# Reversing GpSimd's additions of weight chunks, and placing the last chunks of slots eight and nine anew

## The chip, the core and the metric

The kernel runs on one core of a Trainium2 chip. The metric is the device time of one execution in microseconds (us); the time before is the median of three runs. A core has five engines with a queue each: TensorE (PE in the profile), VectorE (DVE), ScalarE (ACT), GpSimd (POOL) and SyncE (SP), which here only issues transfers (DMAs). An engine takes its instructions in order; it waits on semaphores that other engines and transfers raise.

## The reference, cut to what matters

A thresholded attention (8 batches, 8 heads, 576 tokens, 64 features a head), whose output is the input of a feed-forward block with normalisation in front. The q, k, v and x arithmetic is float32; the weights of the block arrive as float64.

```python
scores = scale * np.matmul(q, k.transpose(0, 1, 3, 2))
thresh = np.max(scores, axis=-1, keepdims=True) - tau
scores = np.where(scores >= thresh, scores, -1000000000.0)
scores = scores - np.max(scores, axis=-1, keepdims=True)
attn = np.exp(scores)
attn = attn / (np.sum(attn, axis=-1, keepdims=True) + 1e-09)
attn_out = np.matmul(attn, v)
# (B,H,S,D) -> (B, S, H*D) = x
xn = (x - mu) / np.sqrt(var + 1e-06) * g_ln
out = x + np.maximum(xn @ w_ch1, 0.0) @ w_ch2
```

## The kernel before, in words

The program is written out by hand in the order of its instructions (a manual schedule), in 72 "slots" of four quarters each: nine slots for each of the eight batches. Slot n is about half the query rows of a pair of heads (the fifth slot of a batch gathers the last rows of all pairs). The same slots carry the feed-forward of earlier tokens: `second_part(n, i)` is called in each quarter and issues matmuls of the feed-forward between those of the attention, as many as a quota allows.

A slot of the attention goes like this. TensorE makes the scores in PSUM (L421). VectorE reduces them to the negated row maximum `neg` (L435), GpSimd makes the threshold `thr` from it (L439), ScalarE the exponentials (L449). VectorE masks them and sums them up (L456, it reads the scores from PSUM) and takes the reciprocal `den` (L461). GpSimd divides (L472). VectorE transposes the result in 32 by 32 blocks into `et` (L546). SP writes `et` to a scratch tensor in DRAM (`scr`, L553, L557) and reads it back as `em` and `er` (L567, L571, L576); in the next slot TensorE multiplies it with the values (L615, L625) and the slot after that ScalarE copies the product (L638) into `x`, whose feature sums GpSimd adds up (L667). In between VectorE turns the next q and k (`turn`, L372 to L382) after GpSimd has scaled q (L354).

**The weights.** The two weight matrices come as 64 bit words and are made float32 on the chip in 32 chunks of 128 x 512 elements (class `Weights`). Chunks 0 to 15 are the first matrix, 16 to 31 the second. A chunk goes through these steps, each counted by a number of its own:

- `fetch` (L257): SP loads the raw words into a free room (`hidden`, a part of `w2`, `x_room`, `y_room`, `stage`, `e`).
- `begin`: VectorE makes the upper bits with two instructions (L273, then L277 with two inputs in SBUF); two ScalarE instructions are noted for later, the low word (L283) and the square of the top (L286, which waits for L277, since both read or write the same room).
- `flush`: issues the noted ScalarE instructions. `first_part` calls it with a limit of one after each of its activations (L813), `carry_all` with none.
- `carry` (L298): GpSimd adds the low word to the upper bits of the chunk.
- `mask` (L304): VectorE sets the values that are too small to zero. Then the room is free for the next fetch, and, for the second matrix, the chunk is ready for TensorE.
- `scale` (L314): GpSimd multiplies chunks of the first matrix with `g_ln`.

`begin_to(most)` begins all fetched chunks below `most`; `carry_all` adds all begun ones, `mask_all` masks all added ones. Their places in a slot are: `mask_all` and `begin_to(masks_at)` in front of L456; `carry_all` right behind `second_part(n, 1)`; then L456 and L472; `mask_all` and `begin_to(behind_at)`; `second_part(n, 2)`; `carry_all`; `turn_blocks` (the transposes L546 and the writes of `scr`); `drip` (leftovers of the feed-forward); and at the end of the slot `begin_to(end_at)` and `carry_all`. The numbers `masks_at, behind_at, end_at` are those of the table `BEGUN`, a row for each slot, the last row for all that follow.

Two consumers matter. `second_plain`, the second product of the first group of tokens, takes chunk 16 + 4m + d/4 for its output part m and its row block d; its last part (m = 3) takes chunks 28 to 31 and runs in slots nine and ten. In its midst stand the mean of the second group (`mean_of`, a matmul with the sums of L667) and, on VectorE, the centred `xc` (`centre`, L690). The first product of the second group on `xc` follows it on TensorE.

In the profile every matmul through `product` has line L101 (two matmuls of 64 columns each, in two records each); `p` is a feed-forward product, `sc` the scores and value products.

Of the kernel before, what the change touches and what calls it, by code (L numbers as in the profile page):

```python
# [18 lines left out]
def kernel(  # L19
# [43 lines left out]
    SLOTS = 2 * HP + 1  # L63
# [113 lines left out]
    class Weights:  # L177
# [113 lines left out]
                most -= 1  # L291
                self.on_scalar.pop(0)()

        def carry(self):
            i = self.carried
            self.carried += 1
            ai = self.chunks[i][0].bitcast(I32)
            nc.gpsimd.tensor_tensor(out=ai, in0=ai, in1=self.words(i, I32)[:, :, 0], op=ALU.add)  # L298

# [30 lines left out]
                    break  # L330

        def carry_all(self):
            self.flush()
            while self.carried < self.begun:
                self.carry()

        def mask_all(self):
            while self.masked < self.carried:
# [8 lines left out]
    def by_blocks(n):  # L347

        return n >= FIRST

    def scale_q(u, q_in):

        for at in (slice(0, 8), slice(8, NB)) if u == 0 else (slice(0, NB),):
            nc.gpsimd.tensor_scalar(  # L354
                out=q_in[:, at], in0=q_in[:, at], scalar1=scl_sb, scalar2=1.0,
                op0=ALU.mult, op1=ALU.mult,
            )
# [46 lines left out]
    def scores(b, s):  # L404


        hp, half = (s, 0) if s < HP else (s - HP - 1, 1)

        pieces = []
        for h in range(2):  # L410
            t = 0
            for j in range(2):
                first = FREE + j * S
                for at, n in span(first, S):
                    pieces.append((t, h, j, at, n, at - first))
                    t += n
        for t, h, j, at, n, o in sorted(pieces):
            r = slice(64 * h, 64 * h + 64)
            for i in range(2):
                qT, kT, ql = turned[b * HP + (2 * j + i if s == HP else hp)]  # L420
                nc.tensor.matmul(  # L421
                    sc[h][64 * i : 64 * i + 64, at : at + n],
                    lhsT=ql[r] if s == HP else qT[r, half, j * 128 + 64 * i : j * 128 + 64 * i + 64],
                    rhs=kT[r, o : o + n], start=True, stop=True,
                )

    def exponentials(n):


        neg = small.tile([128, 4], F32, tag="neg", name="neg")  # L430
        thr = small.tile([128, 4], F32, tag="thr", name="thr")
        es = e_room[(n + 1) % 2 if n <= FIRST else 0]
        for h in range(2):
            i = slice(2 * h, 2 * h + 2)
            nc.vector.tensor_reduce(  # L435
                out=neg[:, i], in_=pairs[h],
                axis=AXL.X, op=ALU.max, negate=True,
            )
            nc.gpsimd.tensor_scalar(  # L439
                out=thr[:, i], in0=neg[:, i], scalar1=-1.0, scalar2=low_sb,  # L440
                op0=ALU.mult, op1=ALU.add,
            )
            if h == 0:
                run(n, "copy")
                conversion.scale_all()
        for i in range(4):
            if i == 2:
                yield es, thr
            nc.scalar.activation(es[:, i], blocks[i], func=AF.Exp, bias=neg[:, i : i + 1])  # L449
# [265 lines left out]
    def run_first(calls):  # L715
        for fn in calls[:1]:
            calls.pop(0)
            fn()

    def run_all(calls):  # L720
        now = calls[:]
        calls.clear()
        for fn in now:
            fn()
# [284 lines left out]
    def run(n, i):  # L1009
        for fn, args in later_calls.pop((n, i), ()):  # L1010
            fn(*args)
# [8 lines left out]
    def second_part(n, i):  # L1020

        nonlocal issued, owed, part, now
        part, now = i, QUARTERS * n + i
        if not queue:
            return
        at = QUARTERS * n + i
        g = sum(issued >= e for e in ends)
        left = sum(ROOM[t % QUARTERS] for t in range(at, ready(g + 1))) if g + 1 < NG else 0
        owed += (ends[g] - issued) * ROOM[i] / left if left > 0 else 8


        steps = 0
        got = 1 if i in (0, QUARTERS - 1) else 2
        while queue and (owed >= 0.5 or got == 1 and i in (0, QUARTERS - 1)):
            got, cost = next(queue[0], (None, 0))
            if got is None:
                queue.pop(0)
                got = 1
            elif got == 0:
                owed = 0.0  # L1040
                break
            else:
                issued += cost
                owed -= cost
                steps += 1
                if steps == 4 and among:
                    mean_of(among[0])
                    centre(among.pop())
# [11 lines left out]
    conversion = Weights()  # L1060
    if w_ch1.dtype == I64:
        conversion.fetch(2)
    else:
# [11 lines left out]

    BEGUN = [
        (0, 0, 2), (3, 3, 4), (5, 5, 6), (7, 7, 8), (9, 9, 10), (11, 11, 12),
        (15, 18, 18), (20, 23, 23), (25, 28, 28), (30, 32, 32),
    ]

    def constants(times):

        warm = ps_ff.tile([128, QH], F32, tag="ff", name="warm")
        for _ in range(times):
            product(warm[:, :128], lhsT=avg_sb, rhs=ident, start=True, stop=True)
# [6 lines left out]
    for n in range(NS):  # L1092
        b, s = divmod(n, SLOTS)
        masks_at, behind_at, end_at = BEGUN[min(n, len(BEGUN) - 1)]
        run(n, -3)
        if 0 < n <= HP:
            constants(8 if n > 1 else 26)
        scores(b, s)
        run(n, -2)
        run(n, -1)  # L1100
        if n == FIRST + 1:
            conversion.take(e_room[1])
        if n + 1 < HP:
            scale_q(n + 1, loaded[n + 1][0])
        rest = exponentials(n)
        es, thr = next(rest)
        run(n, 0)
        if n == HP + 2:
            next(rest, None)
        if n >= HP:  # L1110
            conversion.fetch(3)
        run_first(stores)
        second_part(n, 0)
        while drops and drops[0][0] is nc.gpsimd:
            drops.pop(0)[-1]()
        next(rest, None)

        u = (n + 1) // SLOTS * HP + (n + 1) % SLOTS
        if (n + 1) % SLOTS < HP and u < len(units):
            turn(u)  # L1120
            if u + 1 < len(units) and u != 2:
                load_qk(u + 1 if u > 1 else 3)
        if n < HP:
            conversion.fetch(2 if n else 1)
        if n < SLOTS + HP:
            run_all(aside)
        conversion.mask_all()
        conversion.begin_to(masks_at)
        if n <= HP + 1:
            conversion.carry_all()  # L1130
            conversion.scale_all()
        run(n, 1)
        second_part(n, 1)
        conversion.carry_all()
        conversion.scale_all()
        blocks_go = by_blocks(n)
        diags = weights(es, thr, blocks_go)
        run_all(aside)
        drip()
        if n < SLOTS:  # L1140
            run_all(stores)
        conversion.mask_all()
        conversion.begin_to(behind_at)
        run(n, 2)
        second_part(n, 2)
        conversion.carry_all()
        box = []
        if blocks_go:
            conversion.fetch(3, wait=0)
            scr = turn_blocks(b, s, es)  # L1150
            at_quarter(n + 1, 0, lambda b=b, s=s, scr=scr, box=box: box.append(fetch(b, s, scr)))
        else:

            made = turn_weights(s, es, diags)
            for i, at in enumerate(
                (-1, -1, 0, 0)
            ):
                if i < 3:
                    at_quarter(n + 1, at, next, made)
                else:  # L1160
                    at_quarter(n + 1, at, lambda made=made, box=box: box.append(next(made)))
        at_quarter(
            n + 1, 1 if b == 0 and s <= HP else 3,
            lambda b=b, s=s, box=box: values_of(b, s, box[0]),
        )
        if s in (HP, 2 * HP):
            group_ready(2 * b + (s > HP))
        run_all(aside)
        drip({nc.vector: 4, nc.gpsimd: 6})
        if HP <= n < FIRST:  # L1170
            conversion.fetch(3)
        run(n, 3)
        if b == 0 and s < HP - 1:
            load_v(s + 1)
        elif n >= SLOTS - 2 and (n + 2) % SLOTS < HP and n < NS - 2:
            load_v((n + 2) // SLOTS * HP + (n + 2) % SLOTS)
        second_part(n, 3)
        conversion.begin_to(end_at)
        conversion.carry_all()
        run_all(aside)  # L1180
        drip({nc.vector: 2, nc.gpsimd: 0})
# [40 lines left out]
```

## Time and profile before

| what | value |
|---|---|
| time, median of 3 runs (lowest to highest) | 1358.58 us (1358.57 to 1358.76) |
| the profiled execution's own time | 1360.19 us |
| its span in the profile | 1358.1 us |
| mean granted TensorE clock | 0.995 |
| TensorE busy in 100:120 / 120:140 / 140:160 / 160:180 us, 20 each | 18.4 / 14.9 / 18.1 / 13.0 us |
| TensorE busy in 195.3:1358.0 us | 1150.5 of 1162.7 us |
| VectorE busy in 103.4:126.2 / 126.2:150.5 / 150.5:172.6 us | 22.5 of 22.8 / 22.7 of 24.3 / 21.4 of 22.1 us |
| additions L298, all 32 | first at 19.6, last at 169.5 us |

The three stretches of VectorE's row are slots seven, eight and nine, taken from the start of one slot's reduction L435 to the next one's. Slot six's reduction starts at 76.3 us, slot ten's at 172.6. The conversion of the weights is over at about 179 us; the remaining 1180 us aren't touched by the change except through the time at which they start.

How to read the lines: a line of the timeline is start, duration, engine, source line, operation, output<-input, shapes and count, with the idle time in front of it and what ended it in brackets. A line of the waits is engine, what waited, `<-` what it waited for, then the total in us, how often, and the longest.

### The profile page before, as it was taken

To read this page: it belongs to the slowest core of one execution; us is meant where nothing else is said; L and a number is where in the kernel's file an instruction comes from. 1 tells how busy PE (TensorE), PEld (TensorE's weight loads), DVE (VectorE), ACT (ScalarE), POOL (GpSimd) and SP (SyncE) were. 2 spreads that over 40 slices of the span, in tenths; PEclk is the share of its full clock that TensorE was granted. 3 is DMA by queue.
4 is the path that set the end of the run, shared out by engine and by line. 5 is a ranking of instruction groups with operands and counts; after the bars stand their busy time and mean duration, and the time that the engine had idled before them with its cause. 6 is when DMAs were issued, how large, how long until landed. Compare 5 with 4: busy or idle time off the path is not lost.

```text
span 1358.1 us, 40472 instructions
## 1 busy us (share of the span) xinstructions
PE 1320.2 (97%) x17400; PEld 993.8 (73%) x17400; DVE 885.2 (65%) x1544; ACT 459.3 (34%) x995; POOL 630.0 (46%) x836
## 2 busy tenths in 40 slices
PE   8998889999999999999999999999999999999997
PEld 6764547868677686867768686776868677686957
DVE  7989967766755675666766667556756667666112
ACT  4875333232332323232332323323232323323120
POOL 3566645444534444444443445344444444435313
PEclk9999989999999999999999999999999999999999
DMA  8917875457644566437744577446764476344211
GB/s 156 288 43 194 211 191 160 141 167 200 185 150 146 175 176 198 142 129 189 200 126 159 158 196 189 150 146 180 177 192 142 130 190 181 125 159 136 84 18 20
DMA packets 335299, 213.94 MB, mean 158 GB/s; under 512 B 247376, under 2 KB 292688, under 8 KB 327056
## 3 DMA queue, kind: packets, MB, share of 16 engines
q1 hardware_dynamic: 329008, 210.46, 53.9%
q8 instruction: 137, 2.24, 0.7%
q10 hardware_dynamic: 5952, 0.74, 0.4%
q0 software_dynamic: 160, 0.15, 0.1%
q14 instruction: 42, 0.34, 0.1%
HBM read 124.00 MB, written 87.29 MB: 156 GB/s over the span
## 4 chain that ended last, share of the span: by engine, by line
PE 87%; DVE 3%; DMA 3%; SPq 3%; ACT 2%; issue 1%; POOL 0%; POOLq 0%; DVEq 0%; ACTq 0%
PE p L101 34%; PE seg L101 30%; PE sc L421 10%; PE sc L615 8%; PE sc L625 2%; DVE e L456 1%; ACT e L449 1%; DMA em<-scr 1%; PE tp L101 1%; SPq L118 1%; DMA k_in<-in_k_dram 1%; DVE et L546 1%; PE mean L101 1%; SPq L553 1%; PE var L101 0%
## 5 line engine op out<-in xcount | busy, mean ns | idle before, releaser
L101 PE MATMUL p<-xc,w 128*64 128x288 f32 x4096 | 517.8, 408 | 7.7 <-ACT part L901 4.6
L101 PEld LDWEIGHTS p<-xc,w 128*64 128x64 f32 x4096 | 286.9, 137 | 216.4 <-issue 14.3
L435 DVE TENSOR_REDUCE neg<-sc 128x2 f32<-128x1152 f32 x144 | 188.6, 1351 | 280.4 <-PE sc L421 280.4
L472 POOL TENSOR_SCALAR e<-e,den 128x576 f32<-128x576 f32 x264 | 207.1, 796 | 138.9 <-DVE den L461 138.9
L101 PE MATMUL seg<-hidden,w 128*64 128x144 f32 x3840 | 247.9, 287 | 0.0
L101 PEld LDWEIGHTS seg<-hidden,w 128*64 128x64 f32 x3840 | 234.9, 137 | 11.5 <-issue 8.5
L456 DVE SCALAR_TENSOR_TENSOR e<-sc,thr,e 128x576 f32<-128x576 f32 x288 | 222.3, 809 | 17.3 <-POOL thr L439 11.6
L439 POOL TENSOR_SCALAR thr<-neg,low_sb 128x2 f32<-128x2 f32 x144 | 41.6, 289 | 380.1 <-DVE neg L435 379.3
L813 ACT ACTIVATE hidden<-p 128x288 f32<-128x288 f32 x256 | 106.2, 416 | 294.2 <-PE p L101 294.2
L449 ACT ACTIVATE e<-sc,neg 128x576 f32<-128x576 f32 x288 | 197.4, 754 | 2.4 <-DVE neg L435 2.4
L546 DVE STREAM_TRANSPOSE et<-e 128x1152 f32<-128x1152 f32 x118 | 161.1, 1373 | 13.8 <-POOL e L472 13.3
L421 PE MATMUL sc<-kT,qT 64*64 64x384 f32 (+3 forms) x2048 | 139.4, 403 | 3.1 <-DVE e L456 2.3
L615 PE MATMUL sc<-em,v_in 128*64 128x128 f32 (+1 forms) x2368 | 131.2, 264 | 6.5 <-DMA em<-scr 5.2
L615 PEld LDWEIGHTS sc<-em,v_in 128*64 128x64 f32 x2368 | 123.5, 138 | 15.8 <-DVE w L273 2.6
L101 PE MATMUL seg<-hidden,stage 128*64 128x144 f32 x1920 | 123.3, 286 | 0.0
L101 PEld LDWEIGHTS seg<-hidden,stage 128*64 128x64 f32 x1920 | 117.6, 137 | 2.9 <-issue 2.9
L638 ACT COPY x<-sc 128x128 f32<-128x128 f32 x120 | 31.6, 265 | 246.8 <-PE sc L421 175.1
L886 POOL TENSOR_TENSOR hidden<-hidden 128x576 f32<-128x576 f32 x60 | 84.8, 1427 | 52.0 <-ACT hidden L813 42.4
L421 PEld LDWEIGHTS sc<-kT,qT 64*64 64x64 f32 x2048 | 76.0, 133 | 44.1 <-issue 21.4
L901 ACT COPY part<-seg 128x288 f32<-128x288 f32 x74 | 29.8, 403 | 190.6 <-PE seg L101 190.2
L886 DVE TENSOR_TENSOR hidden<-hidden 128x576 f32<-128x576 f32 x60 | 51.2, 888 | 51.5 <-PE seg L101 48.5
L822 POOL TENSOR_TENSOR hidden<-hidden 128x288 f32<-128x288 f32 x48 | 38.9, 809 | 54.7 <-ACT hidden L820 52.2
(132 smaller groups left out, 1099.2 us busy)
## 6 DMA issues: line engine op xcount, KB each, us to landing
scr<-et SPq DMA_DIRECT2D x63, 1152.0 KB, 4.9
em<-scr SPq DMA_DIRECT2D x63, 1024.0 KB, 5.8
out_dram<-ot SPq DMA_DIRECT2D x248, 36.0 KB, 3.8
q_in<-in_q_dram SPq DMA_DIRECT2D x120, 72.0 KB, 2.8
er<-scr SPq DMA_DIRECT2D x132, 64.0 KB, 5.2
k_in<-in_k_dram SPq DMA_DIRECT2D x116, 72.0 KB, 3.0
v_in<-in_v_dram SPq DMA_DIRECT2D x28, 256.0 KB, 5.4
w<-in_moe_w_ch_dram SPq DMA_DIRECT2D x11, 512.0 KB, 6.3
```

Source lines behind the costliest of these rows:

```text
L101: nc.tensor.matmul(out[r], lhsT=lhsT[:, r], rhs=rhs, **flags)
L421: nc.tensor.matmul(sc[h][64 * i : 64 * i + 64, at : at + n], lhsT=ql[r] if s == HP else qT[r, half, j * 128 + 64 * i : j * 128 + 64 * i + 64],
L435: nc.vector.tensor_reduce(out=neg[:, i], in_=pairs[h], axis=AXL.X, op=ALU.max, negate=True,)
L439: nc.gpsimd.tensor_scalar(out=thr[:, i], in0=neg[:, i], scalar1=-1.0, scalar2=low_sb, op0=ALU.mult, op1=ALU.add,)
L449: nc.scalar.activation(es[:, i], blocks[i], func=AF.Exp, bias=neg[:, i : i + 1])
L456: nc.vector.scalar_tensor_tensor(out=es[:, i], in0=blocks[i], scalar=thr[:, i : i + 1], in1=es[:, i], op0=ALU.is_ge, op1=ALU.mult, accum_o ...
L472: nc.gpsimd.tensor_scalar(out=es[:, i], in0=es[:, i], scalar1=den[:, i : i + 1], scalar2=1.0, op0=ALU.mult, op1=ALU.mult,)
L546: nc.vector.transpose(et[:, :, 64 * h : 64 * h + 64].rearrange("p n (j c) -> p j n c", j=2), es[:, 2 * h : 2 * h + 2].rearrange("p j (n c) ...
L615: nc.tensor.matmul(dst[64 * h : 64 * h + 64], lhsT=vt[:, h, c, :], rhs=pick(em[:, 2 * j : 2 * j + 2, c], h), start=c == 0 and first, stop= ...
L813: nc.scalar.activation(hidden[:, d], p1, func=AF.Relu)
L822: nc.gpsimd.tensor_tensor(out=sq[:, 0], in0=sq[:, 0], in1=sq[:, c], op=ALU.add)
L886: eng.tensor_tensor(out=out[at], in0=in0[at], in1=in1[at], op=op)
```

## The change

Three things. `carry` takes the number of the chunk, and `carry_all` adds the begun chunks from the last to the first instead of from the first to the last. The rows of `BEGUN` for slots eight and nine let one more chunk be begun in front of L456 and one more at each later place of slot eight. And in slot nine (`SLOTS` is 9) there is one more `mask_all` behind the transposes `turn_blocks` and `drip`, in front of the last quarter.

```diff
-        def carry(self):
-            i = self.carried
-            self.carried += 1
+        def carry(self, i):
             ai = self.chunks[i][0].bitcast(I32)
             nc.gpsimd.tensor_tensor(out=ai, in0=ai, in1=self.words(i, I32)[:, :, 0], op=ALU.add)
...
         def carry_all(self):
+
+
             self.flush()
-            while self.carried < self.begun:
-                self.carry()
+            for i in reversed(range(self.carried, self.begun)):
+                self.carry(i)
+            self.carried = self.begun
...
     BEGUN = [
         (0, 0, 2), (3, 3, 4), (5, 5, 6), (7, 7, 8), (9, 9, 10), (11, 11, 12),
-        (15, 18, 18), (20, 23, 23), (25, 28, 28), (30, 32, 32),
+        (15, 18, 18), (20, 23, 23), (26, 29, 29), (31, 32, 32),
     ]
...
         drip({nc.vector: 4, nc.gpsimd: 6})
         if HP <= n < FIRST:
             conversion.fetch(3)
+        if n == SLOTS:
+            conversion.mask_all()
         run(n, 3)
```

What this makes of the queues, chunk by chunk: TensorE and SP keep their order. On GpSimd the additions of one `carry_all` stand in reverse: 1, 0 in slot zero; 14, 13, 12 and 17, 16, 15 in slot six; 19, 18 and 22, 21, 20 in slot seven; 25, 24, 23 and 27, 26, then 28 alone in slot eight; 30, 29, then 31 alone in slot nine. (Before: 23, 24, then 25 to 27 in slot eight, and 28, 29, then 30, 31 in slot nine.) The first of such additions waits for the last chunk's L277 and L283, and a mask of the first chunk waits for the last of the additions. In slots zero to five, but for the pair in slot zero, a `carry_all` finds a single chunk, and nothing moves. On VectorE chunk 25 is begun in front of slot eight's L456, chunk 28 at the end of slot eight (before: in front of slot nine's L456), chunk 30 in front of slot nine's L456 and chunk 31 alone behind it. The masks of chunks 29 and 30 stand behind slot nine's L456, and that of chunk 31 behind slot nine's transposes; before, the masks of 30 and 31 stood in slot ten behind its reductions and transposes.

## The prediction

> **What bounds the kernel now.** I read four views in this order: the page, the waits of TensorE before and after 200 us, the timelines of the engines from 84 to 190 us, and TensorE's granted clock over single stretches. The page gives TensorE 97% of the span, so most of the run can only follow it. The waits say where it doesn't have work:
>
> ```profile
> PE 1320.2 (97%) x17400; PEld 993.8 (73%) x17400; DVE 885.2 (65%) x1544; ACT 459.3 (34%) x995; POOL 630.0 (46%) x836
> ...
> PE p L101 <- DVE w L304: 5.2, 1, 5.2
> PE sc L615 <- DMA em<-scr: 5.0, 3, 2.4
> PE p L101 <- ACT hidden L813: 5.0, 5, 2.5
> ...
> PE p L101 <- ACT part L901: 4.6, 8, 0.6
> PE sc L615 <- DMA em<-scr: 0.2, 1, 0.2
> ```
>
> The three middle lines are of 0 to 200 us, the last two of 200 us to the end: there TensorE waits 4.8 us in 1158. What it gains before 200 us should therefore come out at the end nearly whole. The longest single wait is on a mask (L304). Its neighbourhood, TensorE first, then VectorE:
>
> ```profile
> 169.85 3.13 PE L101 MATMUL p<-hidden,w 128*64 128x288 f32 x24
> 178.21 3.15 PE L101 MATMUL p<-hidden,w 128*64 128x288 f32 x12 [5.22 <-DVE w L304]
> 181.14 1.17 PE L101 MATMUL mean<-sum,avg_sb 128*64 128x288 f32 x4
> 182.10 3.27 PE L101 MATMUL p<-hidden,w 128*64 128x288 f32 x20
> 185.21 4.53 PE L101 MATMUL p<-xc,w 128*64 128x288 f32 x36
> ...
> 172.58 2.61 DVE L435 TENSOR_REDUCE neg<-sc 128x2 f32<-128x1152 f32 x2
> 177.50 0.65 DVE L304 SCALAR_TENSOR_TENSOR w<-stage,w 128x512 f32<-128x512 f32 x1
> 178.08 0.68 DVE L304 SCALAR_TENSOR_TENSOR w<-e,w 128x512 f32<-128x512 f32 x1
> ...
> 173.00:178.20 5.20, 0.00 (x0) 0.85 0.88 264
> 178.20:181.00 2.80, 2.79 (x12) 0.50 0.86 289
> 181.00:183.00 2.00, 2.00 (x10) 0.50 1.17 274
> ```
>
> The masks of chunks 30 and 31 stand in slot ten, behind its reductions and transposes. TensorE stops at 172.98 for chunk 30's. The last three lines (stretch, TensorE busy, granted clock, DMA) show what the stop costs besides: half clock until about 183. Twelve records take 3.15 us; elsewhere 12 take 1.62.
>
> [...]
>
> ```profile
> 132.91 0.69 DVE L277 SCALAR_TENSOR_TENSOR w<-e,w 128x512 uint32<-128x512 uint32 x1
> 133.98 1.72 DVE L277 SCALAR_TENSOR_TENSOR w<-e,w 128x512 uint32<-128x512 uint32 x1
> 133.84 1.30 POOL L298 TENSOR_TENSOR w<-w,e 128x512 int32<-128x512 int32 x1 [4.00 <-DMA scr<-et]
> 135.92 1.30 POOL L298 TENSOR_TENSOR w<-w,e 128x512 int32<-128x512 int32 x1 [0.78 <-DMA v_in<-in_v_dram]
> ```
>
> The second L277 takes 1.72 us instead of 0.69 because an addition runs from 133.84. The next addition lies under L456 (reads PSUM), which keeps its 0.80; so do the 1.33 transposes (L546) and the reductions. [...] Here a 5.2 us gap gave 0.50, one of 4.1 us (137.9 to 142, six records in it) 0.68 over the next 5.3 us, and one of 2.5 us (before 129.4) none.
>
> **The change part by part.** The queues of both programs have the same TensorE and SP order, so only the arrival of operands changes.
>
> (a) Reverse order, slots 0 to 5: one addition at a time but for slot 0, where two swap. The pair waits for chunk 1's L283 (20.0 to 20.7) instead of starting at 19.6, so ends 1.1 us later, at about 23.3. Mask 0 is at 23.75 and VectorE then waits 1.39 us for a DMA anyway. Nothing.
>
> (b) Slot 6, a cost. Additions 12, 13, 14 run from 90.45 to 94.72. Now the first needs chunk 14's L283 (90.94 to 91.6), so they end at 91.6 + 3 x 1.3 = 95.5, and mask 12, which waited for the first of them at 91.8, waits for the last. From 95.5 VectorE has three masks (0.61 apart when alone) and three begun chunks (0.45 + 0.61 each), 5.0 us; GpSimd one scaling (0.69) and four divisions L472 (0.73), 3.6. Where these two met before (96.33 to 100.5) VectorE did 2.9 us of such work and GpSimd 2.2 in 4.2 us, rates of 0.69 and 0.52. So VectorE ends near 102.8 and the transposes L546 start 2.3 us late (100.51 before). L277 of chunk 15 ends at 99.8 instead of 97.7; ScalarE's L286 and the activation L813 behind it move by 2.1, TensorE's gap at 98.4 grows from 0.5 to about 2.6, and neg of slot 7 starts at about 105.5 (103.38). By the gaps above 2.6 us shouldn't halve the clock, but it is near.
>
> (c) Slot 7, paid back. Before, L277 of chunks 21 and 22 took 1.72 and 1.68, blocked by additions; now they take 0.69: 2.0 us less. With 2.1 late at the start, L546 begins at about 123.8 (123.60). TensorE is late by the same, but its matmul at 129.39 waits for L813 behind slot 8's first exponentials, so it resumes at about 129.6; the 3.4 us that it waited there (0.87 + 2.50) cover it.
>
> (d) Slot 8, chunks 23 to 25 in front of the masks L456. VectorE begins three chunks in 3 x 1.06 = 3.2 us; two of them with the blocked 1.72 took 3.16 from 132.46. L456 starts at about 135.9 (135.62). GpSimd's three additions begin behind ScalarE's L283 of chunk 25, near 136.3, and end at 140.2, under L456. Mask 23 waits for the last: VectorE stands from 139.2 to 140.2, a new wait of 1.0. The divisions stand behind the additions. Then VectorE 3 masks and 2 begun chunks, 1.83 + 2.12 = 3.95 us, against four divisions, 2.92: at the rates of (b) 5.7 us, so L546 begins at 145.9. Before it was 146.21: two blocked L277 (1.67 each) and 1.1 go, three chunks shrink to two, the wait comes. Bounds: 144.5 if VectorE is hardly blocked[...]. SP sends scr, then em, at this pace, and the value matmul of slot 8, which waited for em until 163.92, starts at about 163.6.
>
> Chunk 28 is begun after L727, about 148.9. Its transfer was issued at 143.9 and took 4.4 us, landed at 148.3: no wait, though with 0.6 us of cover. It takes 1.1 to 1.5; neg of slot 9 starts at about 150.8 (150.48).
>
> (e) Slot 9. Begun chunks 29, 30 take 2.1 (3.1 before). L456 starts at 159.3 (159.92), additions 30, 29 end at 162.2, masks 29, 30 follow L456 at 163.1 to 164.6 unhindered by a wait. Chunk 31 waits for its transfer: issued at 160.41 with 5.5 us to landing, 0.3 earlier now, so 165.6 to about 167.0. L546 begins at 166.9 (169.33). The addition of chunk 31 runs under it; behind the transpose L733 mask 31 (0.65) is the moved mask_all. If L546 gained nothing, it would delay neg of slot 10 by 0.65 and nobody behind it before the mean. Net: neg of slot 10 at 171.0 (172.58).
>
> (f) TensorE from slot 8's value matmul. From 163.92 before, it had scores at 167.8 and was at 172.98 with chunks 28 and 29. From 163.6 that is 172.7. Chunk 30 is ready: 1.62. Mean: neg 171.0 + 1.3, copy 0.3, GpSimd's sum 0.8, so 173.4 + 0.2, against TensorE's 174.3: no wait; 0.66. Twenty records 2.70. First matmul on xc at 172.7 + 1.62 + 0.66 + 2.70 = 177.7. xc itself: 5.0 us behind neg as before (172.58 to 177.5) is 176.0, first piece at 176.5. Against 185.21: 7.5 us gained, 5.2 of the stop, 2.0 of half clock, 0.3 of (d). Next on TensorE is slot 9's value matmul at 182.5; em was issued at 177.03 with 5.6 to land (182.7), now 2.4 earlier. Covered.
>
> The sum against the profiled execution's own time: 1360.19 - 7.5 = 1352.7 (span 1358.1 to 1350.6). I give 0.2 back for waits behind 185 us. The median of the three runs is 1.61 below the profiled one, so 1358.58 - 7.3 = 1351.3.
>
> **Rivals.**
> 1. Slot 6 isn't paid back. If its TensorE gap of 2.6 halves the clock for some 4.6 us as the long gap did, 2.3 more are lost and scores of slot 7 come at +4.4; or (d) ends at 147.2. For it: slots 7 to 9 have VectorE busy 19 of 20 us, little room. Against: 3.4 us of TensorE waiting before 129.4. A delay at (d)'s L546 reaches 163.92 one for one: 1.3 to 3.5 late, time 1352.9 to 1355.1; I put 1354.
> 2. The stop moves rather than goes: TensorE, free at chunk 30, waits for the sum of slot 10. It decides if neg of slot 10 starts later than about 172. With neg as late as 174, the mean is at 176.6 instead of 174.3, 2.3 lost: 1353.6. Against: VectorE had no idle before 172.58 and loses blocked time.
> 3. The additions, now in one block in front of the divisions, hold each slot's L546, and slots never recover. Price at most 3 x 1.3 us in slots 6, 7, 8 and 2 x 1.3 in slot 9, 14.3 in all. Slower than before by more than 0.2% from 10.1 us on (7.4 of gain and 2.7); at three quarters of the price, 10.7, 1361.9. Against: VectorE has the begun chunks to do meanwhile, and L277 gets back 1 us for each addition moved.
> 4. No change that counts: losses of 4.6 to 10 us between 1 and 3, or the gain lost behind 200 us; 1358.5. The 4.8 us of waits there speak against it.
>
> **How the numbers follow.** Likeliest, 1349.5 to 1352.9: 0.66. Rivals 1 and 2, still faster by over 0.2%, 0.23 together. Rival 4 0.05, rival 3 0.06. A measurement tells some 0.2%, 2.7 us, from no change. Faster 0.89, same 0.05, slower 0.06. The range goes from 1349.3 (VectorE hardly blocked in (d): 1.4 more, and 0.6) to 1355.5, which takes in rival 1's end.
>
> **What would show it.** Right: no TensorE wait on L302's mask line near 173, TensorE's clock 1.0 from 164 to 190, first matmul on xc near 177.7, L277 near 0.69 in slots 7 to 9, L546 at about 102.8, 123.8, 145.9 and 166.9. A new VectorE wait of 1.0 for an addition near 139.5, and one in slot 6 longer than 4.3. Wrong: L546 of slot 8 later than 148, a half clock in slot 7, or a new wait on the mean, on em<-scr or on chunk 28's or 31's transfer that is longer than 2 us.

## The result, and the profile after

| | median us | lowest to highest | runs |
|---|---|---|---|
| before | 1358.58 | 1358.29 to 1358.96 | 5 |
| after | 1353.03 | 1352.05 to 1355.44 | 5 |

The ratio after to before is 0.9964 (95% interval 0.9949 to 0.9978): 5.6 us gained of the 7.3 forecast; the interval lies below 1, so the change is faster. The 1353.03 us lie inside the range of the prediction (1349.3 to 1355.5), but 0.1 us above its likeliest part (1349.5 to 1352.9), where the times of rival 1 begin. The profiled execution of after is the longest of its five, 1355.44 us with a span of 1353.6, so its trace shows a bad draw of the same program. Further down the program was profiled once more, at 1353.26 us; that trace is called "after again".

In the program after, the addition is L296, the mask L302, the scaling L312; most other lines are one higher than before (L436 neg, L457, L473, L547, L616, L814). TensorE's share on the page, then its waits, of which the last line is of 200 us to the end, the others of 0 to 200 us:

```profile
PE 1320.4 (98%) x17400; PEld 993.8 (73%) x17400; DVE 877.9 (65%) x1544; ACT 458.8 (34%) x995; POOL 630.3 (47%) x836
```

```profile
PE p L101 <- ACT hidden L814: 5.5, 4, 2.5
PE sc L616 <- DMA em<-scr: 3.7, 2, 2.3
...
PE sc L616 <- DVE e L457: 1.4, 1, 1.4
...
PE p L101 <- ACT o L853: 0.6, 1, 0.6
...
PE p L101 <- ACT part L902: 4.6, 8, 0.6
```

The line for the mask (5.2 us, one wait) is gone. Behind 200 us TensorE waits 4.6 us, as little as before. In all thirteen profiles of this document the span behind the first matmul on `xc` is between 1172.3 and 1173.2 us: the rest of the run follows the start one for one. VectorE's timeline of after:

```profile
24.18 0.45 DVE L382 STREAM_TRANSPOSE qT<-qk_room 128x256 f32<-128x256 f32 x1 [1.15 <-POOL qk_room L355]
...
95.27 2.31 DVE L302 SCALAR_TENSOR_TENSOR w<-w,w 128x512 f32<-128x512 f32 x3 [7.95 <-POOL w L296]
...
102.26 2.62 DVE L547 STREAM_TRANSPOSE et<-e 128x1152 f32<-128x1152 f32 x2
106.74 2.62 DVE L436 TENSOR_REDUCE neg<-sc 128x2 f32<-128x1152 f32 x2 [1.85 <-PE sc L422]
...
123.52 0.69 DVE L277 SCALAR_TENSOR_TENSOR w<-stage,w 128x512 uint32<-128x512 uint32 x1
...
124.59 0.69 DVE L277 SCALAR_TENSOR_TENSOR w<-stage,w 128x512 uint32<-128x512 uint32 x1
...
141.86 1.84 DVE L302 SCALAR_TENSOR_TENSOR w<-e,w 128x512 f32<-128x512 f32 x2 [0.92 <-POOL w L296]
```

The first line is a new wait in slot one, for GpSimd's scaling of q behind the reversed pair of slot zero. The second is slot six's price: mask 12 now waits for the last of three additions, 7.95 us. The two L277 at 0.69 are slot seven's gain (1.72 and 1.68 before). The last is the new wait of slot eight, 0.92. Between slot six's line and slot seven's stands something that wasn't forecast: `neg` of slot seven at 106.74 waits 1.85 us for scores, where it had waited 0.24 before. TensorE's timeline shows why, and its windows (stretch, length, busy time and records, granted clock, DMA share, GB/s) confirm it:

```profile
100.58 3.65 PE L101 MATMUL p<-xc,w 128*64 128x288 f32 x16 [2.46 <-ACT hidden L814]
...
131.00 10.15 PE L101 MATMUL p<-hidden,w 128*64 128x288 f32 x68 [2.02 <-ACT hidden L814]
...
142.80 1.75 PE L616 MATMUL sc<-em,v_in 128*64 128x128 f32 x28 [1.43 <-DMA em<-scr]
...
165.28 2.66 PE L616 MATMUL sc<-em,v_in 128*64 128x128 f32 x28 [2.31 <-DMA em<-scr]
167.66 2.98 PE L101 MATMUL p<-hidden,w 128*64 128x288 f32 x16
...
172.89 4.59 PE L101 MATMUL p<-hidden,w 128*64 128x288 f32 x36
177.31 0.65 PE L101 MATMUL mean<-sum,avg_sb 128*64 128x288 f32 x4
...
180.94 4.59 PE L101 MATMUL p<-xc,w 128*64 128x288 f32 x36 [0.55 <-ACT o L853]
```

```profile
98.00:110.00 12.00, 8.81 (x78) 0.86 0.29 67
...
150.00:170.00 20.00, 16.25 (x138) 0.91 0.86 217
170.00:190.00 20.00, 19.45 (x214) 1.00 0.84 228
```

From 172.89 on TensorE runs through all 36 records of the last part and the mean without a stop at full clock; that is the change's purpose, reached. But sixteen records take 3.65 us at 100.58 and 2.98 at 167.66, where 2.16 and 2.14 are usual, and 28 value records 2.66 instead of 1.75. The half clock that used to follow the stop is gone with it, and half clock follows two other gaps instead. A third spell of it, behind 131.00 (0.50 from 131.81 to 135.22; 68 records in 10.15 us, 8.47 before), costs nothing: the value matmul behind it still waits 1.43 us for `em`. A spell of before, at slot seven's value matmul (0.50 from 142.51 to 145.92 us), likewise shows no cost: slot nine's `neg` waited for no scores.

Cut at the starts of VectorE's reductions (read off its timeline), the way to the first matmul on `xc` is:

| stretch, us | before | forecast | after | after again |
|---|---|---|---|---|
| start of slot 6's `neg` | 76.31 | 76.31 | 76.11 | 76.27 |
| slot 6, to slot 7's `neg` | 27.07 | 29.2 | 30.63 | 29.00 |
| slot 7 | 22.77 | 20.9 | 21.01 | 21.02 |
| slot 8 | 24.33 | 24.4 | 24.69 | 24.70 |
| slot 9 | 22.10 | 20.2 | 20.56 | 19.94 |
| slot 10's `neg` to `xc` matmul | 12.63 | 6.7 | 7.94 | 7.91 |
| first matmul on `xc` | 185.21 | 177.7 | 180.94 | 178.84 |

The forecast column is the differences of the times that the prediction names; for slot eight's `neg`, which it doesn't name, 126.4 is taken, 2.6 us behind its L546 at 123.8 as before. Between the first two profiles 4.27 us are gained up to `xc`, 0.23 behind it and 0.25 outside the span, together the 4.75 between 1360.19 and 1355.44.

### The profile page after: what moved, and what is told of

Same layout as the page of the kernel before. It is cut to its first block, busy times and chain, and to the rows that moved or that the text cites. A ratio compares the mean times of both kernels' runs of the same rounds, so it can differ in the third digit from the quotient of the medians.

```text
span 1353.6 us, 40455 instructions
## 1 busy us (share of the span) xinstructions
PE 1320.4 (98%) x17400; PEld 993.8 (73%) x17400; DVE 877.9 (65%) x1544; ACT 458.8 (34%) x995; POOL 630.3 (47%) x836
## 4 chain that ended last, share of the span: by engine, by line
PE 87%; SPq 1%; issue 1%; DMA 1%; DVE 0%; POOL 0%; ACT 0%; POOLq 0%; ACTq 0%; DVEq 0%
PE p L101 36%; PE seg L101 31%; PE sc L422 9%; PE sc L616 8%; PE sc L626 2%; PE var L101 1%; PE mean L101 1%; DMA em<-scr 0%; SPq L554 0%; ACT part L902 0%; SPq L118 0%; DMA k_in<-in_k_dram 0%; DVE et L547 0%; POOL w L296 0%; POOL out_dram L745 0%
## 5 line engine op out<-in xcount | busy, mean ns | idle before, releaser
L436 DVE TENSOR_REDUCE neg<-sc 128x2 f32<-128x1152 f32 x144 | 188.6, 1351 | 282.4 <-PE sc L422 282.4
L473 POOL TENSOR_SCALAR e<-e,den 128x576 f32<-128x576 f32 x264 | 209.5, 805 | 133.6 <-DVE den L462 133.6
L457 DVE SCALAR_TENSOR_TENSOR e<-sc,thr,e 128x576 f32<-128x576 f32 x288 | 222.3, 809 | 17.3 <-POOL thr L440 11.6
L814 ACT ACTIVATE hidden<-p 128x288 f32<-128x288 f32 x256 | 106.2, 415 | 295.6 <-PE p L101 295.6
L547 DVE STREAM_TRANSPOSE et<-e 128x1152 f32<-128x1152 f32 x118 | 161.1, 1372 | 14.3 <-POOL e L473 13.7
L616 PE MATMUL sc<-em,v_in 128*64 128x128 f32 (+1 forms) x2368 | 130.9, 264 | 5.2 <-DMA em<-scr 3.7
L616 PEld LDWEIGHTS sc<-em,v_in 128*64 128x64 f32 x2368 | 123.4, 138 | 14.0 <-DVE o L728 2.5
```

Of the source, the lines that this page charges most:

```text
L436: nc.vector.tensor_reduce(out=neg[:, i], in_=pairs[h], axis=AXL.X, op=ALU.max, negate=True,)
L457: nc.vector.scalar_tensor_tensor(out=es[:, i], in0=blocks[i], scalar=thr[:, i : i + 1], in1=es[:, i], op0=ALU.is_ge, op1=ALU.mult, accum_o ...
L473: nc.gpsimd.tensor_scalar(out=es[:, i], in0=es[:, i], scalar1=den[:, i : i + 1], scalar2=1.0, op0=ALU.mult, op1=ALU.mult,)
L547: nc.vector.transpose(et[:, :, 64 * h : 64 * h + 64].rearrange("p n (j c) -> p j n c", j=2), es[:, 2 * h : 2 * h + 2].rearrange("p j (n c) ...
L616: nc.tensor.matmul(dst[64 * h : 64 * h + 64], lhsT=vt[:, h, c, :], rhs=pick(em[:, 2 * j : 2 * j + 2, c], h), start=c == 0 and first, stop= ...
L814: nc.scalar.activation(hidden[:, d], p1, func=AF.Relu)
```

## The experiments

All ran beside the kernel before (medians 1358.37, 1358.44 and 1358.53 us in the three batches). A difference in us is to the median of its own batch. The theory at the outset: the places of the last masks carry most of the gain, the reverse order gains in slot seven and costs in slot six.

**The order alone, the places alone.** First, the changed kernel with the additions in the old order:

```diff
-            for i in reversed(range(self.carried, self.begun)):
+            for i in range(self.carried, self.begun):
```

> The changed kernel with the additions of a carry_all in forward order again; the new table rows and the mask_all of slot nine stay. Theory (the places bring the gain; the reverse order costs in slot 6 and pays in slots 7 to 9): slots 6 and 7 as in the kernel before, neg of slot 8 near 126, no half clock between 98 and 108 us; in slot 8 the blocked L277 and one more begun chunk put L456 near 137.7 and L546 near 147.7, the stop at 173 us is gone; about 1353 us (1351.5 to 1354.5). Rival (the reverse order brings the gain, since L277 isn't blocked any more): 1357 us or more.

Measured 1354.06 us, ratio 0.9968 (0.9956 to 0.9981), 4.3 us gained. Slot six is back at 27.07 us, and slot seven at 22.76: its L277 are blocked again (1.72, 1.68).

Second, the kernel before with the reverse order and nothing else (the change's `carry(i)` and its `reversed` loop).

> The kernel before with the reverse order alone; table and masks at their old places. Theory: the stop of about 5 us for the mask of chunk 30 in slot 10 stays, with the half clock behind it; slot 6 costs 2 to 4 us of which the later slots pay back most; 1357.5 to 1361 us. Rival (the reverse order brings the gain): 1354 us or less.

Measured 1357.39 us over 13 runs, ratio 0.9996 (0.9987 to 1.0004): no change that can be told. The profile is of the shortest of these runs, 1356.22. TensorE's timeline has the stop untouched, though 2 us earlier:

```profile
176.22 3.08 PE L101 MATMUL p<-hidden,w 128*64 128x288 f32 x12 [5.24 <-DVE w L302]
...
182.04 4.53 PE L101 MATMUL p<-xc,w 128*64 128x288 f32 x36
```

In this profile slots six and seven take 29.01 and 21.03 us: +1.94 and -1.74, a trade at par. From the stop's end to `xc` it is 5.82 us, where the prediction's full-clock terms make 1.62 + 0.66 + 2.70 = 4.98. So, by these terms, half clock behind the stop cost 0.84 here, against 2.02 in the profile before (185.21 - 178.21 = 7.00).

Third, the kernel before with the additional `mask_all` of slot nine alone (old order, old table):

```diff
+        if n == SLOTS:
+            conversion.mask_all()
         run(n, 3)
```

> The kernel before with the mask_all of slot nine alone: forward order, old table, the masks of chunks 30 and 31 behind slot nine's transposes. Theory (the stop at 173 us is what there is to gain): the masks end near 173.5, TensorE hardly waits for chunk 30, neg of slot 10 starts 1.3 us later, so the mean waits for its sum until about 176.5 and the first matmul on xc starts near 180 (185.2 before); 1352.5 to 1355 us. Rival (the table and the order are needed as well): 1357 us or more.

Measured 1354.02 us, ratio 0.9967 (0.9954 to 0.9979): these two lines alone give 4.35 of the change's 5.6 us, and as much as the masks and the table together in the first experiment. TensorE's timeline:

```profile
172.87 1.68 PE L101 MATMUL p<-hidden,w 128*64 128x288 f32 x12 [0.32 <-DVE w L304]
176.27 0.71 PE L101 MATMUL mean<-sum,avg_sb 128*64 128x288 f32 x4 [1.73 <-POOL sum L667]
...
179.95 0.46 PE L101 MATMUL p<-xc,w 128*64 128x288 f32 x2 [0.55 <-ACT o L852]
```

As expected, the stop shrinks to 0.32, and the mean becomes late by 1.73 instead. That is the prediction's rival 2, in a kernel without the other parts: here `neg` of slot ten stands at 173.71, later than the 172 from which the rival was to decide, and in after again it is at 170.93, with no wait.

**Reverse order from a slot on.** The changed kernel with the old order up to slot six, the reverse one from chunk 18 (slot seven) on:

```diff
-            for i in reversed(range(self.carried, self.begun)):
+            span = range(self.carried, self.begun)
+            for i in reversed(span) if self.carried >= 18 else span:
```

> The changed kernel with the forward order for chunks 0 to 17 (slots 0 to 6), reverse from chunk 18 on. Theory (slot 6 with its TensorE gap and the half clock behind it is what keeps the change from its full gain): no VectorE wait of 8 us and no TensorE gap of 2.5 us in slot 6, neg of slot 7 near 103.4, of slot 8 near 125, L546 of slot 8 near 145.5 to 146; 1350.5 to 1352 us and little spread between runs. Rival (slot 6 is hidden by TensorE's wait before slot 8, and the rest is lost in slot 8 or behind): the same as the changed kernel, 1352.5 to 1354 us.

Measured 1349.47 us, ratio 0.9936 (0.9924 to 0.9949): 8.9 us faster than before, the fastest kernel of this study. VectorE's and TensorE's timelines of it (most lines stand one higher still, L548, L815):

```profile
90.65 4.07 DVE L302 SCALAR_TENSOR_TENSOR w<-w,w 128x512 f32<-128x512 f32 x3 [4.27 <-POOL w L296]
...
99.36 2.62 DVE L548 STREAM_TRANSPOSE et<-e 128x1152 f32<-128x1152 f32 x2
```

```profile
97.71 2.16 PE L101 MATMUL p<-xc,w 128*64 128x288 f32 x16 [0.50 <-ACT hidden L815]
...
158.06 0.44 PE L617 MATMUL sc<-em,v_in 128*64 128x128 f32 x4 [1.51 <-DVE e L458]
160.16 1.75 PE L617 MATMUL sc<-em,v_in 128*64 128x128 f32 x28 [1.66 <-DMA em<-scr]
161.71 2.14 PE L101 MATMUL p<-hidden,w 128*64 128x288 f32 x16
```

Mask 12 waits 4.27 us for the first addition instead of 7.95 for the last, and the transposes start 2.9 us earlier than in after, 0.95 of them because slot six itself starts earlier (75.16). Slot six takes 27.06 us again while slot seven keeps its 21.01: slot seven's gain doesn't need slot six's price. TensorE's gap in front of 97.71 is 0.50 instead of 2.46.

The same with the reverse order only from chunk 23 (slot eight) on, `>= 23` in the diff above:

> The changed kernel with the forward order for chunks 0 to 22 (slots 0 to 7), reverse from chunk 23 on. Theory (VectorE's blocked L277 count in every one of slots 7 to 9, since VectorE sets the pace there): slot 7 loses its 2.0 us of unblocked L277 again, neg of slot 8 comes about 2 us later than with forward order to slot 6; 1351 to 1352.5 us. Rival (only slots 8 and 9 count, slot 7 has time to spare): 1349 to 1350 us, as with forward order to slot 6.

Measured 1352.05 us, ratio 0.9951 (0.9938 to 0.9963), 2.5 us less gain than from chunk 18, as the theory had it. Slot seven takes 22.79 us: 1.78 of the 2.5 are its blocked L277.

The reverse order from chunk 18 on in the kernel before, with its old table and no additional masks:

> The kernel before with the reverse order from chunk 18 on (slots 7 to 9), table and masks at their old places. Theory (order and places act one after the other on the same chain: the order brings slot 10's start forward, the places take the stop out of slot 10, so the gains add): the stop of 5 us stays but begins 3 to 4 us earlier; 1353 to 1354.5 us. Rival (the stop hides what the order gains, as it stood in the way in the run with the reverse order alone): 1356.5 us or more.

Measured 1354.90 us over nine runs, ratio 0.9974 (0.9964 to 0.9983), 3.5 us gained, 0.4 less than the theory's range allowed and far from the rival's 1356.5. The stop remains, and slots seven, eight and nine take 21.02, 23.59 and 20.41 us:

```profile
174.38 3.15 PE L101 MATMUL p<-hidden,w 128*64 128x288 f32 x12 [4.85 <-DVE w L302]
...
180.92 4.53 PE L101 MATMUL p<-xc,w 128*64 128x288 f32 x36
```

So the reverse order moves everything earlier but leaves the stop in place; half clock behind it cost 180.92 - 174.38 - 4.98 = 1.56.

**What the table is worth.** The same kernel with the additional `mask_all` as well, and the old table:

> The kernel before, old table of places, with two edits: from chunk 18 on the begun chunks are added in reverse order, and slot nine's last masks stand behind its turning (mask_all when n == SLOTS). Against the forward-to-slot-six version (e3) only the table rows of slots eight and nine differ. Theory (the table rows are worth nothing by themselves; slot seven's order and the masks carry the gain): 1349.5 to 1351.5, first matmul on xc 174 to 176 us. Rival (the rows are what lets the reverse order pay in slots eight and nine): 1352.5 to 1354, first matmul on xc near 177 to 178, with a wait of over 2 us for a chunk of slot eight or nine that the trace of the kernel after doesn't show.

Measured 1350.74 us, ratio 0.9941 (0.9928 to 0.9953), 7.8 us gained: the sum of 3.5 and 4.35 for its two parts. The kernel with the new table ran beside it on the same chip:

> The same kernel as e3_forward_to_slot6 on the same chip as the one above, for the comparison: 1349 to 1351.

Measured 1351.14 us, ratio 0.9943 (0.9931 to 0.9956). The rows of `BEGUN` are worth nothing that the medians can tell. In the old table's profile slots eight and nine take 23.63 + 21.77 = 45.40 us, in the new one's 24.77 + 20.56 = 45.33: the same work, moved. What the rows may still bring is hidden by the clock: the old table's profile has no half clock between 98 and 190 us (1.00 in every window) and a wait of 1.34 us of the mean for its sum, the new one's has no such wait but half clock at slot eight's value matmul (0.91 over 150 to 170 us), which cost it 1.67 us.

A third row for slot eight, (26, 26, 29), leaves its last chunks to the end of the slot, so that the transposes go earlier:

```diff
-        (15, 18, 18), (20, 23, 23), (26, 29, 29), (31, 32, 32),
+        (15, 18, 18), (20, 23, 23), (26, 26, 29), (31, 32, 32),
```

> Forward order to slot 6, reverse from chunk 18 on, and slot 8's row (26, 26, 29): chunks 26, 27 and 28 are all begun behind slot 8's transposes L547. Theory (slot 8's value matmul waits for em, and em for these transposes): L547 of slot 8 starts about 2 us earlier, TensorE's wait of 1.7 us for em in slot 9 goes; but three additions in a block stand in front of GpSimd's q scaling in slot 9, so neg of slot 10 doesn't come earlier and the mean waits for its sum instead: 1349 to 1350.5 us, no clear gain. Rival (em alone sets the time there): 1347.5 to 1348.5 us.

Measured 1352.08 us, ratio 0.9951 (0.9937 to 0.9964); both expectations missed, it is 2.6 and 0.9 us slower than the two measurements of the version it was made from. VectorE's timeline:

```profile
140.63 2.82 DVE L548 STREAM_TRANSPOSE et<-e 128x1152 f32<-128x1152 f32 x2
...
153.69 0.77 DVE L378 STREAM_TRANSPOSE qT<-q_in 128x256 f32<-128x256 f32 x2 [2.67 <-POOL q_in L356]
```

The transposes are 2.4 us earlier (143.02 without this row), as meant. But, as the theory had named, the additions now stand in front of GpSimd's scaling of q (L356), and VectorE waits 2.67 us for that; `neg` of slot ten gains nothing (93.71 us behind slot six's, 92.77 and 93.38 in the version it was made from).

**Slot six's price: VectorE or the clock?** The changed kernel, with ScalarE's two instructions for chunk 15 left behind slot six's L814 instead of in front of it, so that TensorE's matmul needn't wait for VectorE's late L277:

```diff
-            conversion.flush(1)
+            if not 15 <= conversion.carried < 18:
+                conversion.flush(1)
```

> The changed kernel (reverse order everywhere) with ScalarE's L283 and L286 of chunk 15 behind slot 6's last activation L813 of that quarter instead of in front of it, so that TensorE isn't held by chunk 15 while VectorE is as late as in the changed kernel. Theory (part of slot 6's loss is the TensorE gap and the half clock behind it): no gap of 2.5 us near 98 us, clock 1.0 from 98 to 108, neg of slot 7 directly behind L547 near 105; 1351 to 1352.3 us, with less spread between runs than the changed kernel. Rival (VectorE's wait for the additions alone costs the 3.6 us): the same as the changed kernel, 1352.7 to 1353.7 us.

Measured 1351.67 us, ratio 0.9953 (0.9941 to 0.9966). TensorE's timeline in slot six:

```profile
96.45 3.56 PE L101 MATMUL p<-xc,w 128*64 128x288 f32 x28
...
103.34 2.16 PE L101 MATMUL p<-xc,w 128*64 128x288 f32 x16 [1.00 <-ACT hidden L814]
...
108.01 10.15 PE L101 MATMUL p<-xc,w 128*64 128x288 f32 x68 [2.02 <-ACT hidden L814]
```

The gap of 2.46 is down to 1.00, but the next one, in front of 108.01, has grown to 2.02 (0.75 in after): the gap has moved rather than gone, and half clock follows it: the clock is 0.97 over 98 to 110 us and 0.93 over 110 to 129, and the 68 records take 10.15 us (8.47 at full clock). Slot six still takes 28.73 us, 0.27 less than in after again, without any half clock in it, so the slot's price is VectorE's. The spell behind 108.01 costs nothing that shows: slot seven takes 21.06 us. The median lies 1.4 us under the 1353.03 of after, and 2.2 under that of the run below, more than the 0.27 of the slot. This profile has full clock at slot eight's value matmul (1.00 over 147 to 163 and 163 to 172 us), where both profiles of after lose 1.67 us; whether that is the edit's doing or chance isn't shown.

Last, the changed kernel itself on the chip of the third batch.

> The changed kernel itself, beside e3 on one chip. Theory (slot six's order costs it 3 to 4 us, about 1.4 of it by TensorE's half clock): 1352 to 1355.5, 2.5 to 4 us above the forward-to-slot-six version. Rival (the distance between after and e3 was one of chips): within 1.5 us of the forward-to-slot-six version.

Measured 1353.84 us, ratio 0.9964 (0.9951 to 0.9976), 2.7 us above the version with the old order to slot six beside it. TensorE's timeline, and the window of slot six:

```profile
100.76 2.16 PE L101 MATMUL p<-xc,w 128*64 128x288 f32 x16 [2.45 <-ACT hidden L814]
...
161.09 0.44 PE L616 MATMUL sc<-em,v_in 128*64 128x128 f32 x4 [1.20 <-DVE e L457]
163.18 2.80 PE L616 MATMUL sc<-em,v_in 128*64 128x128 f32 x28 [1.65 <-DMA em<-scr]
165.71 2.84 PE L101 MATMUL p<-hidden,w 128*64 128x288 f32 x16
```

```profile
98.00:110.00 12.00, 8.81 (x92) 1.00 0.27 63
```

The same program and the same gap, 2.45 us, and here the clock stays at 1.00: `neg` of slot seven is at 105.27. At slot eight's value matmul half clock came again (0.91 over 150 to 170 us). And the version with the old order to slot six, in its second profile, shows there what its first, with 1.00 over 150 to 170 us, did not (0.91):

```profile
160.79 2.67 PE L617 MATMUL sc<-em,v_in 128*64 128x128 f32 x28 [2.30 <-DMA em<-scr]
163.18 2.97 PE L101 MATMUL p<-hidden,w 128*64 128x288 f32 x16
```

From the value matmul to the one on `er` (L627) its two profiles have 160.16 to 163.78 and 160.79 to 166.08, 3.62 and 5.29 us: 1.67 for a spell of half clock that one execution has and another hasn't.

## Why the prediction was right, and short

*(a) Slots zero to five, nothing: a term that was put at nothing and isn't always.* The pair ends 1.1 us later in its slot, as forecast, and mask 0 holds nothing up. But behind the pair GpSimd scales q, and VectorE waits for that: 1.15 to 1.17 us in all four profiles with slot zero reversed, not in the nine others. In those it waits for the DMA instead, from nothing to 1.55 us. So slot one takes 12.41 to 12.89 us reversed and 11.58 to 12.93 us in the old order: the reversal costs up to 0.8 us when the transfer lands early, and nothing when it lands late. Slot six starts at 76.11 and 76.27 in the two profiles of after, at 76.31 before, and from 75.13 to 76.67 in the ten others.

*(b) Slot six, a cost.* The mechanism and the size are as worked out: L547 at 102.26 and 102.44 (forecast 102.8), the slot 1.94 us longer in after again and with the reverse order alone (forecast 2.1). What failed is the sentence "By the gaps above 2.6 us shouldn't halve the clock": it made a rule of a single gap of 2.5 us. A gap of 2.46 did so in the first profile of after (0.86 over 98 to 110 us; 1.63 us more), and gaps of 2.45 in two other profiles, after again and the reverse order alone, didn't (1.00). Rival 1 named this as its way in; this branch of it came true in one profile of after out of two.

*(c) Slot seven, paid back.* Right: L277 at 0.69, the slot 1.75 shorter. With full clock `neg` of slot eight is at 126.29, forecast 126.4. TensorE resumes at 129.53, forecast 129.6, but behind that gap too half clock followed where none was expected (in after again 12 records at 129.53 took 3.15 us, 1.62 at full clock; 0.92 over 129 to 150). It was luck that it cost nothing: the next value matmul waited for `em` anyway, 1.70 us. That (b) and (c) cancel was forecast; that one could have the second without the first, the forecast didn't ask, and on one chip it is worth 2.7 us. In reverse, the additions start only behind the last chunk's L277, and none runs beside it; in slot six they leave VectorE standing, since mask 12 is its next instruction and waits for all three.

*(d) Slot eight.* The new wait is 0.92 and 0.90 (forecast 1.0), the slot 24.69 and 24.70 (24.4; 24.33 before). L547 stands at 147.50 and 146.03 (145.9). The 147.2 of rival 1 was the author's estimate: about what 140.2 + 3.95 + 2.92 = 147.07 gives, VectorE's work and the divisions one behind the other. No run showed them so. As the experiments with either table show, the new rows neither gain nor lose what a median can tell.

*(e) Slot nine.* L547 at 168.59 and 167.08 (166.9), VectorE waits 0.61 and 0.35 us for chunk 31's transfer, where the forecast's times left 1.0 (164.6 to 165.6). `neg` of slot ten in after again is at 170.93; the forecast was 171.0.

*(f) The last stretch: the term that was mis-sized.* The stop of 5.2 us is gone and rival 2's wait didn't come (in the first profile of after `neg` is as late as 173.00, but TensorE is late by as much). The "2.0 of half clock" isn't all gained. First, 2.0 was one execution's value: the same stop cost 0.84 and 1.56 in two other kernels. Behind the stop's end half clock lasted 5.26 us before (178.21 to 183.47) and there about 2.9 and 4.3, estimates from the 12 records of 3.08 us (1.62 at full clock) and from the clock of 0.61 over 174 to 180 us; half of that is 0.6 more than the cost each time. Second, half clock came at slot eight's value matmul instead (0.91 over 150 to 170 us), and cost 1.67 us in both profiles of after (5.29 us to the matmul on `er`, 3.62 with full clock), where the forecast had TensorE's clock at 1.0 from 164 to 190, one of its signs of being right. From that matmul to the one on `xc` the forecast had 14.1 us (163.6 to 177.7). With full clock the version with the old order to slot six takes 14.02 (160.16 to 174.18), although `xc` waits 0.55 us for a copy of ScalarE (L853 in after); both profiles of after take 15.66.

*The sum.* It was made against the profiled execution (1360.19 - 7.3 = 1352.9; after again took 1353.26), then carried to the median, 1.61 lower, as if an execution at the median had as much to lose as the profiled one. These 1.61 are nearly all of the 1.7 us by which the forecast missed. That the profiled execution before was long by its half clock fits this, but isn't shown, since no other execution of before was profiled. The lengths of the runs of after go with their mean granted clock, 0.998 at 1352.05 us, 0.996 at 1352.68 and 1353.03, 0.995 at 1355.39 and 1355.44; three thousandths of 1353 us are 4.1, the distance of the ends is 3.4.

Rival 1 has its half clock and its late slot seven in the first profile of after, as said, but not in the second. Rival 3, the additions holding every L547, showed its mechanism in slot six and with 0.9 us in slot eight; slots seven and nine got shorter. Rival 4 didn't come.

What stays open: the version with the old order to slot six is faster than after by 3.6 us, measured on two chips, and by 2.7, side by side on one. On the one chip slot six's 1.95 and slot one's 0.82 (12.41 and 11.59 us) make 2.77, though the two profiles, single executions, differ by 1.76 us in all. Fewer spells of half clock may add to it: the runs there have a mean clock of 0.9953 for after and 0.9968 for the version, which by estimate is about one spell an execution (0.0015 x 1352 = 2.0 us, against 1.71 for a spell). Where the spells stood only a profiled execution shows, and there is one for each kernel and batch.

The best version: the additional `mask_all` of slot nine, with the reverse order from slot seven on, at 1349.47, 1350.74 (old table) and 1351.14 us; 1353.03 and 1353.84 for after.

## What to carry to other kernels

An order that is right in one place of a repeated schedule can cost in the next: ask for each place who waits for the first result and whom the work blocks, and apply it only where it pays. Before a gain is counted, take half clock out of the profile's times: here a gap of 2.46 us brought it in one execution, and gaps of 2.45 us at the same place didn't in two others, so the new program may draw anew at each such gap that is left. Look first for finished inputs whose last step stands behind foreign work on its engine (here two masks behind the reductions of the next slot): moving them took two lines and gave most of the gain.

## What the runs showed of the hardware

The length of the gap didn't tell whether half clock followed. Gaps of 2.45 and 2.46 us in slot six went both ways (clock 1.00 and 0.86 over 98 to 110 us), and so did the two waits around four records of slot eight's value matmul: 1.51 and 1.66 us without half clock, 1.20 and 1.65 us with it (1.00 and 0.91 over 150 to 170 us). What separates the executions isn't shown. Between 20 and 1345 us the profiles of before and after have five spells of it:

| profile | clock at 0.50, us | length | TensorE busy in the 3.41 us before |
|---|---|---|---|
| before, slot seven's value matmul | 142.51 to 145.92 | 3.41 | 1.02 |
| before, the stop | 176.64 to 183.47 | 6.83 | 0.00 |
| after, slot six's gap | 101.09 to 104.50 | 3.41 | 0.95 |
| after, the gap before 131.00 | 131.81 to 135.22 | 3.41 | 1.40 |
| after, slot eight's value matmul | 165.94 to 169.35 | 3.41 | 1.10 |

The rest of that time is at 1.00. A spell of 3.41 us takes 1.71 us of TensorE's full-speed time; it cost 1.63 us in slot six and 1.67 at slot eight's value matmul, and nothing where TensorE waited for something else behind it (131.00).

VectorE's instructions took longer beside some of GpSimd's, by more than one amount. L277, with two inputs, took 1.67 to 1.72 us in seven of its 32 cases in before, each with an addition running. In after it took 0.69 or 0.70 in 22 cases, and 1.03 to 1.17 in ten, each beside a division (L473), L668 or L729. GpSimd's instruction grew too: in slot six of after a division starts at 98.97 and takes 1.43 us instead of 0.73, and the L277 behind it starts at 99.90 and takes 1.03. L273, with one input, took 0.40 to 0.44 us in 27 cases of after and 0.84 to 0.96 in five, each of these with a GpSimd instruction running.
